# A third pair of token blocks in seven products, and the weights' conversion moved

## The chip, the cores and the metric

The kernel runs on one core of a Trainium2 chip. The metric is the device time of one execution in microseconds (us); lower is better. Five engines work side by side, each through its own instructions in order: TensorE (PE, matmuls), VectorE (DVE), ScalarE (ACT), GpSimd (POOL) and SyncE (SP, which here issues the DMAs).

## The reference

```python
# N = 6016 tokens, C = 256
qn = q / (norm(q, axis=tokens) + 1e-06);  kn = k / (norm(k, axis=tokens) + 1e-06)
s  = kn.T @ qn / tau                      # 256 x 256, over all tokens
a  = softmax(s);  x = v @ a               # 6016 x 256
h  = maximum(x @ w_in, 0);   x = (h * h) @ w_out              # first MLP, 256 -> 2048 -> 256
xn = x / sqrt(mean(x * x, -1) + 1e-06) * rms_g
g, val = xn @ w_gate, xn @ w_val                              # second MLP, 256 -> 1536
out = (g * sigmoid(g) * val) @ w_out2                         # 1536 -> 256
```

## The kernel before

Tokens are cut into 12 blocks (ten of 512, two of 448 columns), and blocks 2p and 2p+1 make pair p, p from 0 to 5. Features lie on the 128 partitions and tokens on the free axis. The scores come first, in a single pass over q and k; attention's matrix `a` is then multiplied into the first MLP's weights, so that the first MLP works on v directly with the operands `m_h`, `m_l`. Every float32 product is made of three matmuls of rounded parts, high by high, high by low, low by high (`mm3`, L109 to L112); what is "hi" below is a copy by ACT, what is "lo" the difference by DVE.

*First MLP.* A plain block runs 16 units, one for each 128 of the 2048 hidden features: a unit has 12 matmuls, six up and six down. A pair in the other form (`mlp1_pair`, L1310) runs 8 groups of two units for both its blocks. In place of eight 128-wide products (four combinations of feature half and input half, for two blocks) a group has seven products of sums and differences of the operands (`A11`, `S1`, ... `S4`), each of three matmuls, 21 for 24, followed by 24 down matmuls. `FIRST` is the first pair in this form: pairs 4 and 5 have it before. Its inputs are seven combinations of the pair's v, each as hi and lo. `v_steps` (L1198) forms them: load, transposes (L1219), differences (L1225, L1240), hi and lo. For the first such pair they stay on the chip (`first_place`), for the next they go through DRAM (`through_dram`) and come back by `fetch_v`. The weights' own sums and differences (`comb_steps`, 16 steps) are made beside the plain blocks, at the units that `COMB` names.

*Between the MLPs.* Each pair's output gets its norm (`pair_norm`, L976 to L1008: squares, a sum over 32 columns, a matmul with `mean_w`, the root, a reciprocal) and is formed into seven operands for the second MLP (`pair_steps`, stored to DRAM as `xd`). Both run as side steps (`side`, `aside`) of a later stage. A side step goes between two products of a group, so it stands in order on its engine among that group's own work.

*Second MLP.* Every pair runs 12 groups of seven products (L1458) and 12 down matmuls. After product 0, ACT copies its bank (L1511), and the next products accumulate onto that copy. The gate and value weights come as float64 halves, 256 columns of the 1536 in a chunk. A chunk takes a load (L134), a scaling on GpSimd and ACT (L142, L145), bit steps on DVE (L153, L157), for the value some sums on GpSimd, and a hi and lo of each piece; `gv_chunk(i)` is a chunk's tile of 1792 KB, and group f uses chunk f//2. Before, all six chunks are converted beside blocks 2 to 6: chunk 0 stays on the chip, and 1 to 5 go to DRAM and are loaded again (chunk 1 at L1766 after group 0 of the last MLP1 pair, 2 to 5 at L1828 after group 0 of the second MLP). The last rows of the second w_out (`late_calls`, tile `pu`) are loaded and converted beside MLP2's pair 0.

*Order.* The program order on each engine is written by hand. `CONV` says beside which blocks conversion steps run, `SKIP` which units take none. All DMAs that the change touches are issued by SP, in the order of the program; SP issues as soon as the waits of the DMA at its head are met.

Of the kernel before, what the change touches and what calls it, by code (L numbers as in the profile page):

```python
# [20 lines left out]
P = 128  # L21
# [7 lines left out]
def attn_moe_kernel(ctx: ExitStack, tc, q, k, v, tau, w_in, w_out, w_gate, w_val, w2, rms_g, out):  # L29
# [26 lines left out]
    FIRST = NP - 2  # L56
# [132 lines left out]
    EARLY = 3  # L189
    gv, gv_dram = {}, {}  # L190
# [11 lines left out]
    class Pieces(Call):  # L202


        def hi_of(self, j):
            src, x, k = self.pieces[j]
            if self.i < HELD:
                dst = gv_chunk(self.i)[:, :, x : x + k]
            else:
                dst = wp.tile([P, 2, 2, W2], F32R, tag="gp", name="gp", bufs=2)[:, :, :k]  # L210
            nc.scalar.copy(out=dst[:, 0], in_=src)
            self.made.append(dst)

        def lo_of(self, j):
# [3 lines left out]
            if self.i >= HELD:  # L218
# [8 lines left out]
        def h(self):  # L227
            self.made = []
            for j in range(self.np):
                self.hi_of(j)  # L230
                if self.i >= HELD:
                    self.lo_of(j)

        def l(self):
            if self.i < HELD:
# [162 lines left out]
    gv_calls = []  # L398
    for i in range(NGV):
        gate = Gate(cols(w_gate, i), i)  # L400
        gv_calls += [gate, Value(cols(w_val, i), i, gate)]
# [796 lines left out]
    def v_steps(p, into):  # L1198
# [11 lines left out]
        def tr(t, kk):  # L1210
            def f():
                if t == 0 and kk == 0:
                    x = vp.tile([P, KC, NB], F32, tag="vt", name="vt")[:, :, :n]
                    st["x"] = {0: x[:, 0], 4: x[:, 1], 5: x[:, 0]}
                if t == 1 and kk == 0:
# [72 lines left out]
    def fetch_v(p, i, ops):  # L1288
# [3 lines left out]
        if k < 6:  # L1292
# [10 lines left out]
    def mlp1_pair(p, ops, side, after_product, after_group):  # L1303
# [10 lines left out]
        def down(f, t, d, ph, pl, first, last):  # L1314
            def g():
# [115 lines left out]
    leftover, pw = [], []  # L1431

    def mlp2(p, ops, after_product, after_group, side):
# [17 lines left out]
        def group(f):  # L1451
            c = gv[f // 2]
# [235 lines left out]
    SKIP = {2: (), 3: (6, 9, 10), 4: (1, 5, 9, 13), 5: (3, 6, 8, 9), 6: (6, 9, 13, 15)}  # L1688
    COMB = {2: (4, 10, 14), 3: (12, 13, 14), 4: (8, 9, 11), 5: (0, 10, 12, 13, 14), 6: (11, 12)}
# [48 lines left out]

    ops0 = {}
# [4 lines left out]
    for p in range(FIRST, NP):  # L1744
        nxt = {}
        last = p == NP - 1
        if not last:
            tokens += v_steps(p + 1, through_dram(p + 1, first_stage))

        def after_product(g, i):  # L1750
            if g == NF1 // 2 - 1:
                if not last and i in ORDER[3:]:
                    fetch_v(p + 1, i, nxt)
                if last and i == 0:
                    fetch(0, 4, ops0)

        def after_group(g):
            if g == 0 and p > FIRST:
                side.extend(pair_norm(p - 1) + pair_steps(p - 1, staged("ys", "p0", "ys", "p1")))
# [4 lines left out]
            if last:  # L1764
                if g == 0:
                    nc.sync.dma_start(out=f32(gv_chunk(1)), in_=gv_dram[1])  # L1766
                if g == NF1 // 2 - 2:
                    assert not side, len(side)
# [122 lines left out]
```

## Time and profile before

| | |
|---|---|
| median of three runs | 1121.04 us (1120.5 to 1121.63) |
| the profiled execution | 1122.16 us |
| its span | 1120.5 us |
| PE busy | 1107.9 us, 99% |
| DVE, ACT busy | 779.8 and 789.6 us, 70% each |
| plain blocks 2 to 7, about | 188 to 437 us of the span |
| pairs 4 and 5 of the first MLP | 437 to 508, 508 to 577 |
| second MLP, pair 0 | 577 to 677; the later pairs about 90 us each |

The span is the time from the first to the last instruction of the profile; the execution's own time has 1.66 us more around it. A timeline row gives the start, the duration and the instruction; consecutive alike instructions are joined as "x6", and their duration then runs from the first start to the last end. An idle stretch ahead of a row stands in brackets with what ended it. Matmuls are pipelined: the next starts before the last has ended, so the pitch is the difference of two starts.

### The profile page before, as it was taken

What the parts mean: (1) busy time and instruction counts of PE and PEld (TensorE: products, weight loads), DVE (VectorE), ACT (ScalarE), POOL (GpSimd) and SP (SyncE); (2) the same over time, 40 slices, a digit from 0 to 9 for tenths busy, and PEclk for the clock granted to TensorE, in tenths of its full rate; (3) what the DMA queues carried; (4) which work ended last, traced back from release to release, by engine and by line L of the source; (5) the groups of instructions that cost most, each with busy time, mean ns of one, the idle gap of its engine ahead of it and who ended that gap; (6) DMA issues with size and microseconds to landing.
All of it is one profiled execution on the core that took longest, in us unless ns stands there. A gap on an engine that the chain in (4) does not pass through costs nothing.

```text
span 1120.5 us, 14578 instructions
## 1 busy us (share of the span) xinstructions
PE 1107.9 (99%) x5170; PEld 931.7 (83%) x5170; DVE 779.8 (70%) x1194; ACT 789.6 (70%) x1428; POOL 74.5 (7%) x106
## 2 busy tenths in 40 slices
PE   8999999999999999999999999999999999999997
PEld 7978888888888888888987888888888888888996
DVE  6998768887878787966857775555555655655655
ACT  7688778888888787777778666656566556556654
POOL 2521102202111000000000000000000000000000
PEclk9999999999999999999999999999999999999999
DMA  9633322362433331352276143102302302202001
GB/s 327 227 113 95 102 66 77 94 216 85 142 141 104 122 102 50 118 182 95 85 261 274 44 172 104 41 1 75 94 1 75 94 1 75 78 10 66 19 19 34
DMA packets 103305, 114.47 MB, mean 102 GB/s; under 512 B 50368, under 2 KB 71872, under 8 KB 102592
## 3 DMA queue, kind: packets, MB, share of 16 engines
q1 hardware_dynamic: 100960, 112.68, 29.8%
q10 hardware_dynamic: 2272, 0.85, 0.3%
q8 instruction: 41, 0.67, 0.2%
q14 instruction: 32, 0.26, 0.1%
HBM read 71.83 MB, written 41.68 MB: 101 GB/s over the span
## 4 chain that ended last, share of the span: by engine, by line
PE 90%; ACT 3%; DVE 2%; DMA 2%; POOL 1%; issue 1%; SPq 0%; DVEq 0%; ACTq 0%
PE mm L1458 29%; PE acc L110 13%; PE acc L112 13%; PE acc L111 13%; PE mm L1351 6%; PE mm L111 5%; PE mm L112 5%; PE mm L110 5%; POOL rows L569 1%; DMA qraw<-in_k_dram 1%; DMA rraw<-in_v_dram 1%; PE mm L761 1%; ACT ws L592 0%; ACT hl L609 0%; DVE dg L153 0%
## 5 line engine op out<-in xcount | busy, mean ns | idle before, releaser
L1458 PE MATMUL mm<-p,gv 128*128 128x512 f32 (+1 forms) x1188 | 302.6, 387 | 0.3 <-ACT mm L1511 0.3
L1458 PEld LDWEIGHTS mm<-p,gv 128*128 128x128 f32 x1188 | 221.6, 188 | 46.4 <-ACT mm L1511 1.4
L1561 DVE TENSOR_TENSOR sh<-hp,sh 128x512 fp32r<-128x512 f32 (+1 forms) x144 | 98.0, 681 | 139.6 <-ACT sh L1557 139.3
L1511 ACT COPY mm<-mm 128x512 f32<-128x512 f32 (+1 forms) x72 | 40.4, 561 | 171.0 <-PE mm L1458 161.9
L110 PE MATMUL acc<-sh,wo_h 128*128 128x512 f32 (+1 forms) x384 | 149.0, 388 | 0.0
L112 PE MATMUL acc<-sh,wo_l 128*128 128x512 f32 (+1 forms) x384 | 148.2, 386 | 0.2
L111 PE MATMUL acc<-sh,wo_h 128*128 128x512 f32 (+1 forms) x384 | 148.3, 386 | 0.0
L849 DVE TENSOR_TENSOR sh<-p,sh 128x512 fp32r<-128x512 f32 x128 | 92.8, 727 | 53.5 <-ACT sh L842 47.3
L110 PE MATMUL acc<-sh,w_h 128*128 128x512 f32 (+1 forms) x284 | 109.5, 386 | 0.0
L112 PE MATMUL acc<-sh,w_l 128*128 128x512 f32 (+1 forms) x284 | 109.5, 386 | 0.0
L111 PE MATMUL acc<-sh,w_h 128*128 128x512 f32 (+1 forms) x284 | 109.5, 385 | 0.0
L837 ACT ACTIVATE p<-mm 128x512 f32<-128x512 f32 x128 | 76.1, 594 | 27.6 <-PE mm L112 27.1
L1557 ACT CAST sh<-hp 128x512 fp32r<-128x512 f32 (+1 forms) x144 | 89.1, 619 | 3.2 <-DVE hp L1545 1.9
L112 PE MATMUL mm<-p,m_l 128*128 128x512 f32 x224 | 87.5, 391 | 0.3 <-DVE m_l L773 0.3
L110 PE MATMUL mm<-p,m_h 128*128 128x512 f32 x224 | 87.3, 390 | 0.0
L111 PE MATMUL mm<-p,m_h 128*128 128x512 f32 x224 | 87.2, 389 | 0.0
L112 PEld LDWEIGHTS acc<-sh,wo_l 128*128 128x128 f32 x384 | 72.1, 188 | 14.5 <-DVE wo_l L182 1.0
L111 PEld LDWEIGHTS acc<-sh,wo_h 128*128 128x128 f32 x384 | 72.1, 188 | 13.3 <-DVE sh L849 0.3
L110 PEld LDWEIGHTS acc<-sh,wo_h 128*128 128x128 f32 x384 | 72.1, 188 | 13.3 <-ACT wo_h L175 0.2
L1458 PE MATMUL mm<-xs,gv 128*128 128x512 f32 (+1 forms) x324 | 82.6, 381 | 0.0
L1545 DVE TENSOR_TENSOR hp<-mm,sg 128x512 f32<-128x512 f32 (+1 forms) x72 | 49.0, 680 | 43.3 <-PE mm L1458 42.9
L1536 DVE TENSOR_TENSOR hp<-mm,pu 128x512 f32<-128x512 f32 (+1 forms) x72 | 49.0, 681 | 30.2 <-ACT pu L1535 30.2
(249 smaller groups left out, 2078.8 us busy)
## 6 DMA issues: line engine op xcount, KB each, us to landing
p<-xd SPq DMA_DIRECT2D x58, 256.0 KB, 4.0
xd<-xp SPq DMA_DIRECT2D x40, 256.0 KB, 2.2
gv<-gvd SPq DMA_DIRECT2D x5, 1792.0 KB, 16.4
gvd<-gp SPq DMA_DIRECT2D x15, 512.0 KB, 3.3
xd<-p SPq DMA_DIRECT2D x30, 256.0 KB, 2.2
raw<-in_moe_w_out_dram SPq DMA_DIRECT2D x11, 512.0 KB, 3.6
out_dram<-ot SPq DMA_DIRECT2D x40, 128.0 KB, 2.3
qraw<-in_q_dram SPq DMA_DIRECT2D x13, 384.0 KB, 7.3
```

The costliest lines, as they stand in the source:

```text
L110: nc.tensor.matmul(o, wh, xh, start=start, stop=False)
L111: nc.tensor.matmul(o, wh, xl, start=False, stop=False)
L112: nc.tensor.matmul(o, wl, xh, start=False, stop=stop)
L837: nc.scalar.activation(out=r, in_=o, func=AF.Relu)
L849: nc.vector.tensor_tensor(out=sl, in0=s, in1=f32(sh), op=ALU.subtract)
L1351: nc.tensor.matmul(bank, m_part(a, w, g), x, start=start and j == 0, stop=j == 2, skip_group_check=not start)
L1458: nc.tensor.matmul(bank, c[:, hl, a, fs], x, start=start and j == 0, stop=j == 2, skip_group_check=not start)
L1511: cp(out=bu, in_=b0)
L1536: add(out=h22, in0=bh, in1=w, op=ALU.add)
L1545: dve(out=h21, in0=bv, in1=sg1, op=ALU.mult)
L1557: nc.scalar.copy(out=parts[t][0], in_=x)
L1561: dve(out=pl, in0=x, in1=f32(ph), op=ALU.subtract)
```

## The change

Pair 3 (blocks 6 and 7) takes the seven-product form too: `FIRST` goes from NP−2 to NP−3, and pairs 3, 4 and 5 have it. What goes with it:

- Conversion beside the plain blocks now ends with block 4, and only chunks 0 to 2 are converted there (`STREAMED = 3`); the 16 combination steps stand in blocks 2 to 4.
- Chunk 3 is converted beside the last MLP1 pair, in `vraw`, `dg`, `vt`, and staged through `p1` and `p6` to DRAM.
- Chunks 4 and 5 are converted beside pair 0 of the second MLP, straight into their tiles. Gate and value loads are new DMAs into tiles named `cr`.
- The operands of pair 5 take the tile `gv1` (as `vx`), so chunk 1's load moves from after group 0 of the last MLP1 pair to after product 1 of its last group.
- The last pair's MLP1 output is parked in DRAM (`yd`, four stores after group 1 of MLP2's pair 0), loaded back in pair 2 (`XLATE`), and its norm and operands are formed from group 3 of pair 2 on.
- `chunk_steps` is called with a list `early`. It is empty, so the loads are ordinary side steps, and `late_loads` is empty.

```diff
-    FIRST = NP - 2
+    FIRST = NP - 3
+    STREAMED = 3
@@ class Pieces
+        def direct(self):
+            return self.i < HELD or self.i > STREAMED
@@ def hi_of
-            if self.i < HELD:
-                dst = gv_chunk(self.i)[:, :, x : x + k]
-            else:
-                dst = wp.tile([P, 2, 2, W2], F32R, tag="gp", name="gp", bufs=2)[:, :, :k]
+            dst = gv_chunk(self.i)[:, :, x : x + k] if self.direct() else self.stage()[:, :, :k]
...
-    for i in range(NGV):
+    gv_calls = [c for i in range(STREAMED) for c in chunk_calls(i)]
@@ v_steps
+        wide = p > FIRST + 1
...
-                raw[t] = load_v(b + t)
+                raw[t] = load_v(b + t, place(0, F32) if wide else None)
...
+                if t == 0 and kk == 0 and wide:
+                    x = wp.tile([P, NC7, NB], F32, tag="gv1", name="vx")
@@ fetch_v
+        if k < 3 and p > FIRST + 1:
+            if k == 0:
+                ops["x"] = wp.tile([P, NC7, NB], F32R, tag="gv1", name="vx")
...
-    SKIP = {2: (), 3: (6, 9, 10), 4: (1, 5, 9, 13), 5: (3, 6, 8, 9), 6: (6, 9, 13, 15)}
-    COMB = {2: (4, 10, 14), 3: (12, 13, 14), 4: (8, 9, 11), 5: (0, 10, 12, 13, 14), 6: (11, 12)}
+    SKIP = {2: (4, 10, 14), 3: (4, 6, 9, 12, 13), 4: (1, 5, 9, 11, 13)}
+    COMB = {2: (2, 4, 6, 10, 14), 3: (0, 2, 12, 13, 14), 4: (2, 8, 9, 10, 11, 12)}
...
+    def chunk_steps(i, homes, early, stage=None):
+        calls2 = chunk_calls(i)
+        steps = []
...
+        gate, value = calls2
+        if early:
+            early.extend([gate.load, value.load])
+        else:
+            steps.append(gate.load)
+        for c in calls2:
+            after = [value.load] if c is gate and not early else []
+            steps += [only("act", c.a), only("dve", seq(c.b0, c.b1)), only("dve", seq(c.b2, *after))]
...
+            for j in range(c.np):
+                steps += [hi(j), only("dve", lambda c=c, j=j: c.lo_of(j))]
@@ the loop over the paired stages
-        if not last:
-            tokens += v_steps(p + 1, through_dram(p + 1, first_stage))
+        if last:
+            tokens += chunk_steps(
+                STREAMED, *shared_homes(), lambda t=cycle((1, 6)): place(next(t)).rearrange("p a (c w) -> p a c w", w=W2)
+            )
+        else:
+            tokens += v_steps(p + 1, through_dram(p + 1, stage if first else staged("p1", "ys")))
...
+                if last and i == 1:
+                    nc.sync.dma_start(out=f32(gv_chunk(1)), in_=gv_dram[1])
...
-                if g == 0:
-                    nc.sync.dma_start(out=f32(gv_chunk(1)), in_=gv_dram[1])
@@ beside the second MLP
-    x, y = rows_steps[1:], pair_side[6:]
-    side += pair_side[:5] + rows_steps[:1] + pair_side[5:6] + [f for i in range(max(len(x), len(y))) for f in x[i : i + 1] + y[i : i + 1]]
+    early, spare = [], {}
+    for i in range(STREAMED + 1, NGV):
+        chunk_side.append(chunk_steps(i, (gate_home, value_home), early))
+    late_loads = early[:2]
+    chunk_side[1][3:3] = [both(*early[2:])]
+    x, y = rows_steps, sum(chunk_side, [])
+    side += [f for i in range(max(len(x), len(y))) for f in x[i : i + 1] + y[2 * i : 2 * i + 2]]
...
-                    for i in (2, 3, 4, 5):
+                    for x in late_loads:
+                        x()
+                    for i in range(2, STREAMED + 1):
                         nc.sync.dma_start(out=f32(gv_chunk(i)), in_=gv_dram[i])
-            if f == 10 and p == 0:
+                if f == 1:
...
+                    for i in range(4):
+                        nc.sync.dma_start(out=y_dram[:, i, :nl], in_=x[:, 2 * i, :nl])
+            if p == XLATE:
...
+                if f == 3:
+                    side.extend(pair_side)
```

SP's queue at the start of the second MLP, before. `w_h` and `w_l` are rows of the second w_out, `gvd` the converted chunks in DRAM, `pu` the raw rows of the late w_out.

```order
L134 DMA pu<-in_moe_w_out_dram 128x2x512 [waits DMAHW0_49,PE_49]
L1808 DMA w_h<-w2d 128x1536 [waits DMAHW1_49,PE_49]
L1808 DMA w_l<-w2d 128x1536 [waits DMAHW2_49]
L1828 DMA gv<-gvd 128x3584 [waits DMAHW3_49]
L1828 DMA gv<-gvd 128x3584 [waits DMAHW4_49]
L1828 DMA gv<-gvd 128x3584 [waits DMAHW5_49,PE_49]
L1828 DMA gv<-gvd 128x3584 [waits DMAHW6_49,PE_49]
```

And the same place after the change:

```order
L134 DMA pu<-in_moe_w_out_dram 128x2x512 [waits DMAHW6_49,PE_49]
L1907 DMA w_h<-w2d 128x1536 [waits DMAHW7_49,PE_49]
L1907 DMA w_l<-w2d 128x1536 [waits DMAHW0_49]
L1933 DMA gv<-gvd 128x3584 [waits DMAHW1_49]
L1933 DMA gv<-gvd 128x3584 [waits DMAHW2_49]
L134 DMA cr<-in_moe_w_gate_dram 128x2x512 [waits DMAHW3_49,Pool_49]
L1938 DMA yd<-xst 128x448 [waits DMAHW4_49,Activation_49]
```

Two chunk loads of four remain, and the gate weights of chunk 4 stand behind them, ahead of the parked state's stores.

ACT's queue where group 1 of MLP2's pair 0 ends and group 2 begins, before:

```order
L1557 CAST sh<-hp 128x512 [waits DVE_49]
L1531 ACTIVATE sg<-mm 128x512 [waits PE_49]
L1535 COPY pu<-mm 128x512 [waits PE_49]
L976 ACTIVATE q<-xst 128x896 [waits DMAHW5_49,DMAHW4_49,Activation_49]
L145 ACTIVATE pu<-pu 128x512 [waits DMAHW0_49]
L1511 COPY mm<-mm 128x512 [waits DVE_49,PE_49]
```

After:

```order
L1578 CAST sh<-hp 128x512 [waits DVE_49]
L1552 ACTIVATE sg<-mm 128x512 [waits PE_49,Activation_49]
L1556 COPY pu<-mm 128x512 [waits PE_49]
L145 ACTIVATE cr<-cr 128x512 [waits DMAHW3_49]
L1532 COPY mm<-mm 128x512 [waits DVE_49,PE_49]
```

The norm's square has left this place; the conversion of the gate load stands where the conversion of the w_out rows was, which is now one group earlier.

DVE's queue in the only paired stage that has a norm beside it before, pair 5 (`p_4840` and `q` are the norm's; L1338 and L1341 the square and the low part of a group's activations; L1399 a sum of two banks):

```order
L981 TENSOR_TENSOR p_4840<-p_4840,q 128x1024
L984 STREAM_TRANSPOSE q<-p_4840 128x1024
L1338 TENSOR_TENSOR p_4015<-p_4014 128x448
L1341 TENSOR_TENSOR sh<-p_4015,sh 128x448
L987 TENSOR_REDUCE ns<-q 128x32
L1338 TENSOR_TENSOR p_4015<-p_4013 128x448
L1341 TENSOR_TENSOR sh<-p_4015,sh 128x448
L1399 ISA p_4013<-mm,sh 128x448
```

The same norm beside pair 4 after the change:

```order
L989 TENSOR_TENSOR p_4055<-p_4055,q 128x1024
L992 STREAM_TRANSPOSE q<-p_4055 128x1024
L1253 TENSOR_TENSOR xp<-vx,xp 128x448
L1357 TENSOR_TENSOR p_3219<-p_3218 128x512
L1360 TENSOR_TENSOR sh<-p_3219,sh 128x512
L995 TENSOR_REDUCE ns<-q 128x32
L1232 STREAM_TRANSPOSE vx<-p_4026 128x448
L1238 TENSOR_TENSOR vx<-vx 128x448
L1357 TENSOR_TENSOR p_3219<-p_3217 128x512
L1360 TENSOR_TENSOR sh<-p_3219,sh 128x512
L1418 ISA p_3217<-mm,sh 128x512
```

The group's own steps are the same, 512 columns wide; three steps of the next pair's preparation stand among them.

## Rows read from the trace of the kernel before

**Rows 1.** The page's first part: busy us, share of the span, instructions.

```profile
PE 1107.9 (99%) x5170; PEld 931.7 (83%) x5170; DVE 779.8 (70%) x1194; ACT 789.6 (70%) x1428; POOL 74.5 (7%) x106
```

**Rows 2.** The chain of waits: share of the span by engine.

```profile
PE 90%; ACT 3%; DVE 2%; DMA 2%; POOL 1%; issue 1%; SPq 0%; DVEq 0%; ACTq 0%
```

**Rows 3.** Windows: stretch, us, busy us of each engine, clock, DMA share, GB/s.

```profile
188.00:230.00 42.00, 42.00 (x188) 34.81 (x187) 38.12 (x54) 36.36 (x65) 12.47 (x13) 1.00 0.31 104
437.00:508.00 71.00, 71.00 (x317) 59.04 (x316) 55.20 (x90) 52.63 (x97) 0.00 (x0) 1.00 0.42 155
508.00:582.00 74.00, 73.96 (x359) 66.63 (x358) 54.02 (x88) 55.98 (x107) 0.15 (x1) 1.00 0.31 111
582.00:677.00 95.00, 94.70 (x414) 76.52 (x413) 67.79 (x109) 68.63 (x129) 1.97 (x3) 1.00 0.47 186
```

**Rows 4.** PE timeline in the second MLP's pair 1.

```profile
705.75 1.52 PE L1458 MATMUL mm<-p,gv 128*128 128x512 f32 x6
707.11 1.52 PE L1458 MATMUL mm<-xs,gv 128*128 128x512 f32 x6
708.47 0.39 PE L110 MATMUL acc<-sh,w_h 128*128 128x512 f32 x1
```

**Rows 5.** DVE timeline in pair 5 of the first MLP, with a norm.

```profile
521.91 1.22 DVE L981 TENSOR_TENSOR p<-p,q 128x1024 f32<-128x1024 f32 x1
523.16 1.25 DVE L984 STREAM_TRANSPOSE q<-p 128x1024 f32<-128x1024 f32 x1
...
530.89 0.63 DVE L1341 TENSOR_TENSOR sh<-p,sh 128x448 fp32r<-128x448 f32 x1 [2.06 <-ACT p L1336]
```

**Rows 6.** PE timeline in pair 5, matmuls of 448 columns.

```profile
531.48 0.36 PE L110 MATMUL acc<-sh,wo_h 128*128 128x448 f32 x1
531.68 0.37 PE L111 MATMUL acc<-sh,wo_h 128*128 128x448 f32 x1
531.89 0.37 PE L112 MATMUL acc<-sh,wo_l 128*128 128x448 f32 x1
```

**Rows 7.** DVE timeline in pair 4, a group without a norm.

```profile
450.84 0.63 DVE L1225 TENSOR_TENSOR p<-p,p 128x448 f32<-128x448 f32 x1
451.38 0.69 DVE L1341 TENSOR_TENSOR sh<-p,sh 128x512 fp32r<-128x512 f32 x1
```

**Rows 8.** PE timeline in pair 4, the matmul on that low part.

```profile
452.39 0.39 PE L111 MATMUL acc<-sh,wo_h 128*128 128x512 f32 x1
```

**Rows 9.** Issues at 579.5, 580.9, 585.0 us: KB each, us to landing.

```profile
pu<-in_moe_w_out_dram SPq DMA_DIRECT2D x1, 512.0 KB, 6.0
gv<-gvd SPq DMA_DIRECT2D x1, 1792.0 KB, 12.8
gv<-gvd SPq DMA_DIRECT2D x1, 1792.0 KB, 17.3
```

**Rows 10.** Windows at the end of pair 5, and after it.

```profile
573.00:580.00 7.00, 7.00 (x34) 5.98 (x33) 4.79 (x9) 5.97 (x11) 0.00 (x0) 1.00 0.55 181
580.00:602.00 22.00, 22.00 (x97) 17.35 (x96) 13.01 (x20) 17.35 (x30) 0.66 (x1) 1.00 1.01 411
```

**Rows 11.** ACT timeline around group 2 of the second MLP.

```profile
592.23 0.69 ACT L145 ACTIVATE pu<-pu 128x512 int32<-128x512 uint32 x1
594.17 0.57 ACT L1511 COPY mm<-mm 128x512 f32<-128x512 f32 x1 [1.25 <-DVE hp L1545]
```

**Rows 12.** PE timeline of the same stretch.

```profile
591.74 2.91 PE L1458 MATMUL mm<-p,gv 128*128 128x512 f32 x12
...
595.17 1.52 PE L1458 MATMUL mm<-p,gv 128*128 128x512 f32 x6
```

**Rows 13.** Windows after the last matmul.

```profile
1113.90:1117.70 3.80, 0.17 (x1) 0.00 (x0) 1.18 (x2) 0.00 (x0) 0.00 (x0) 1.00 0.79 190
1117.90:1120.50 2.60, 0.00 (x0) 0.00 (x0) 0.00 (x0) 0.00 (x0) 0.00 (x0) 0.50 0.26 57
```

**Rows 14.** PE timeline at the start of the span.

```profile
1.19 3.60 PE L584 MATMUL mm<-ws 128*128 128x512 bf16 x8 [1.19 <-DVE ws L580]
```

More of the change, by code (lines that the diff above doesn't have):

```diff
@@ L1211, in f @@
             def f():
-                if t == 0 and kk == 0:
+                if t == 0 and kk == 0 and wide:
+                    x = wp.tile([P, NC7, NB], F32, tag="gv1", name="vx")
+                    st["x"] = {i: x[:, i, :n] for i in range(NC7)}
+                elif t == 0 and kk == 0:
                     x = vp.tile([P, KC, NB], F32, tag="vt", name="vt")[:, :, :n]
                     st["x"] = {0: x[:, 0], 4: x[:, 1], 5: x[:, 0]}
-                if t == 1 and kk == 0:
+                elif t == 1 and kk == 0 and not wide:
                     a, c = (place(k, F32)[:, :, :n] for k in (0, 1))
@@ L1737, in attn_moe_kernel, with seq, g, hi @@
     assert not spill
+    formed = set()
+    def seq(*fs):
+        def g():
+            for f in fs:
+                f()
+        return g
+    def chunk_steps(i, homes, early, stage=None):
+        calls2 = chunk_calls(i)
+        steps = []
+        for c, home in zip(calls2, homes):
+            c.take = lambda c=c, home=home: c.__dict__.update(zip(("raw", "g"), home()))
+            if stage:
+                c.stage = stage
+        gate, value = calls2
[6 more added lines that the diff above has]
+            steps += [only("act", c.a), only("dve", seq(c.b0, c.b1)), only("dve", seq(c.b2, *after))]
+            def hi(j, c=c):
+                def f():
+                    if j == 0:
+                        c.made = []
+                    c.hi_of(j)
+                f = only("act", f)
+                f.staged = bool(stage)
+                return f
+            for j in range(c.np):
+                steps += [hi(j), only("dve", lambda c=c, j=j: c.lo_of(j))]
+        steps[-1] = only("dve", seq(steps[-1], lambda: formed.add(("gv", i))))
+        return steps
+    def flat_tile(pool, tag):
+        k = 2 if tag == "ys" else 1
+        return pool.tile([P, 2, NB], F32, tag=tag, name="cr", bufs=k)
+    def as_raw(t):
+        return t.rearrange("p a n -> p (a n)").bitcast(I32)
+    def shared_homes():
+        return (
+            lambda: (as_raw(flat_tile(vp, "vraw")), wp.tile([P, NB], F32, tag="dg", name="cg", bufs=3)),
+            lambda: (as_raw(flat_tile(vp, "vraw")), flat_tile(vp, "vt")[:, 0]),
+        ), []
     ops0 = {}
@@ L1746, in attn_moe_kernel @@
         last = p == NP - 1
-        if not last:
-            tokens += v_steps(p + 1, through_dram(p + 1, first_stage))
+        first = p == FIRST
+        stage = first_stage if first else staged("ys", "p0", "ys") if last else staged("ys", "p2")
+        if last:
+            tokens += chunk_steps(
+                STREAMED, *shared_homes(), lambda t=cycle((1, 6)): place(next(t)).rearrange("p a (c w) -> p a c w", w=W2)
+            )
+        else:
+            tokens += v_steps(p + 1, through_dram(p + 1, stage if first else staged("p1", "ys")))
         def after_product(g, i):
@@ L1764, in after_group @@
             if last:
[L1765 to L1766 removed]
                 if g == NF1 // 2 - 2:
[L1768 removed]
+                    assert not side and not tokens, (len(side), len(tokens))
                     for i in ORDER[:3]:
@@ L1810, in load_w2 @@
             )
+    XLATE = 2
+    nl = blocks[-1][1]
+    y_dram = dp.tile([P, 4, NB], F32, tag="yd", name="yd")
     ops, nxt, tails = ops0, {}, []
```

48 lines of the change are left out of this document (36 added, 12 removed).

## The prediction

> **What bounds the kernel now.** I read the busy line first: TensorE (PE) is busy 99% of the span, VectorE (DVE) and ScalarE (ACT) 70% each [rows 1]. The chain of waits says the same: 90% of the path that ended last is PE [rows 2]. The table by stage shows where that could change: PE has no gap worth naming in the plain blocks, the two paired stages and the first pair of the second MLP, and beside it DVE is at 78 to 91% in the first two and at 71 to 73% in the others, ACT at 72 to 87% [rows 3]. So a matmul that goes is worth its pitch, and what the other engines or a transfer do costs only where PE comes to wait for it. The pitch is the distance of starts, not the duration of one: twelve matmuls of 512 columns take from 705.75 to 708.47, 0.227 us each [rows 4].
>
> **The change, part by part.** The sum is made against the profiled execution: its own time is 1122.16 us, 1.12 above the median of 1121.04, and its span 1120.5. A sum of differences is added to the median.
>
> PE. Per pair, eight groups of 24 product matmuls in place of 2 × 8 × 12 up matmuls become eight of 21: 24 matmuls of 512 columns go. 24 × 0.227 = −5.45 us; with the small mean matmul of one norm −5.5. I see nothing that could take this back by itself.
>
> Blocks 2 to 4. Here DVE and ACT carry the same chunks' conversion and the combination steps squeezed from five blocks into three. A block is 16 × 12 × 0.227 = 43.6 us of PE. A block and its surroundings now show DVE 38.1 in 42.0 us [rows 3]; summed by the durations of their rows, the three blocks come to some 40, 41 and 38 us after. That still fits, so I take 0, with 1.0 as the upper end for one unit that bunches.
>
> Pair 4, now a middle pair. Its norm, 1024 wide, runs on DVE in front of the products' low parts, and now in the same stretch the next pair's preparation (L1232, L1238, L1253) stands between them. The only row where before does such a norm inside a paired stage is in the last pair: the two wide steps take 1.22 and 1.25 us, and the low part L1341 that follows the chain ends at 530.89 + 0.63 = 531.52 [rows 5], 0.16 us before the matmul that reads it, at 531.68 [rows 6]. Three added steps of 448 columns cost their spacing of 0.54 us each (450.84 to 451.38 [rows 7]), 1.6; the 512-wide forms of nine others some 0.06 each, 0.5. Against that a group of 45 matmuls is 45 × (0.227 − 0.205) = 1.0 longer than at 448 columns [rows 4, 6]. 1.6 + 0.5 − 1.0 − 0.16 = 0.9, say 1.0. The next group has the other half of the chain; a pair's group without a norm has 0.32 of slack (452.07 against 452.39 [rows 7, 8]), which one step more exceeds: 0.4. Together +1.4, from 0.3 (ACT, for which DVE idled 2.06 us in [rows 5], lets it catch up) to 3.0 (DVE's work of the two groups, 12.4 and 10.9 us by rows, against 10.2 us of PE each, all of it unhidden).
>
> Pair 5. The chunk's conversion puts one low part (some 0.6 us) into the same chain with its 0.16 of slack: +0.4, from 0 to 1.5.
>
> First pair of the second MLP, the large term. The new gate load of chunk 4 (512 KB) stands in SP's order behind w2_l and two chunk loads, and ACT's conversion of it (L145) stands directly ahead of group 2's first copy (L1532 now, L1511 before). ACT works in order, so that copy waits for the transfer, and PE's next products accumulate onto what the copy frees. When does it land? Before, the w_out load issued at 579.5 landed 6.0 later, at 585.5; the first chunk load, issued at 580.96, 12.8 later, at 593.8; the third, issued at 585.05, 17.3 later, at 602.3 [rows 9]. That is 4.27 us for each 1792 KB, with the 16 DMA engines full from 580 to 602 (share 1.01 at 411 GB/s [rows 10]). All of these land in the order of issue. Two chunk loads stand before the gate: 593.8 + 4.27 = 598.1. The load of chunk 1, moved from the start of pair 5 to right ahead of this burst, adds 4.27 of transfer; 0.45 × 7.0 = 3.2 us of free share lie in 573 to 580 [rows 10], so it pushes the burst by some 1.1. The gate's own 512 KB take 4.27 × 512/1792 = 1.2. It lands at 598.1 + 1.1 + 1.2 = 600.4, on before's clock.
>
> What needs it: before, L145 there ran at 592.23 for 0.69 us, on a load that had long landed, and the copy at 594.17 for 0.57 [rows 11]; the products followed at 595.17 [rows 12]. Now L145 ends at 601.1 and the copy at 601.6: PE resumes some 6.4 us late. Lower end 5.0 (the moved chunk hides wholly, and PE has 1.3 us more queued work than I count); upper end 8.5 (chunk 1's transfer is hidden by nothing). VectorE waits for the same transfer through GpSimd's scaled half, but its shift is behind the same products, 0.
>
> The Trainium skill speaks against this term ("DMA: Bandwidth & Descriptors", section "Queues, rings and completion order"): descriptors of one queue start in order but are pipelined over 16 engines, and nothing orders DMAs across these. By it the small gate load could end ahead of the chunks. The trace agrees only with order of issue in this burst, so I keep it as a rival.
>
> The w_out load and its L145, now ahead of group 1, landed at 585.5 where PE wanted the copy's input at about 587: 0, up to 1.0 with the push. The value load and chunk 5's loads are issued groups ahead of their use: 0. Parking and reloading pair 5's state are eight transfers of 224 KB with groups between: 0. The norm and its table loads move to MLP2 pair 2 at the same price: 0.
>
> The clock. After the last matmul the granted clock was still 1.00 in 1113.9 to 1117.7 and 0.50 in 1117.9 to 1120.5, with no matmul [rows 13]. It fell some 4 us after PE's last matmul, whose end the first of these stretches holds, and a stall of 6.4 us is longer. What a low clock costs is seen at the start: eight matmuls of 512 columns, the first work after idling, take 3.60 us to the end of the last [rows 14], about 0.427 each with the level at 1.2 GHz, where 2.4 GHz gives 0.227. If it recovers as there, after some 3.9 us, 3.9 × (1 − 0.227/0.427) = +1.8 us; from 0 (the gate doesn't fall) to 3.4 (it stays low twice as long).
>
> The Trainium skill says that the slow level is the default and that activity releases the fast one ("TensorE: Matmul & The Clock Gate", Part 1); by it a stall costs more than its length, as the tail's rows agree. Without it the sum is the same.
>
> Sum: −5.5 + 0 + 1.4 + 0.4 + 6.4 + 1.8 = **+4.5**, so 1121.0 + 4.5 = **1125.5 us**.
>
> **Rivals.** *The gate load lands in time.* If the load's packets pass the chunks', or ACT's L145 is not what the products wait for, the large term and the clock's go and −5.5 + 1.8 = −3.7 remains: 1117.3, faster. It decides when the load has landed by 593.9 (595.17 less 0.69 and 0.57), 6.5 us ahead of what the order of issue gives. For it: PE's slack behind group 1's twelve matmuls [rows 12]; against it: four landings in order at a full share [rows 9, 10]. 12%.
>
> *A short stall.* The load lands late, but the stall stays near 5.0, the clock holds, and the pairs lose little: −5.5 + 5.0 + 0 + 1.0 = +0.5 to +2.0, 1121.5 to 1123.0: no change. For it: the clock outlasts four idle us in the tail. 21%.
>
> *VectorE overloaded in the pairs.* The low parts fall behind in groups 1 to 3 of pair 4 and again in pair 5, at their upper ends 3.0 + 1.5 in place of 1.8: 1125.5 + 2.7 = 1128.2, slower. For it: DVE's 0.16 us of slack [rows 5, 6]; against it: its idle 2.06 us just ahead. It decides once the wide chain has no idle gap to shrink. 12%.
>
> *The saving doesn't come*: the seven products need as many copies and low parts as PE waits for. Against it: pair 4 before has them at PE 71.00 of 71.00 us [rows 3]. 2%, at 1131.
>
> **How the numbers follow.** Forecast 53% (own range 1123.3 to 1127.5), rivals 12, 21, 12 and 2. Differences within 0.2% (1118.8 to 1123.3) can't be told from no change. Faster: the first rival and a little of the second, 13%; same: the second, 21%; slower: the forecast, the third and the fourth, 66%. For 8 in 10 the range leaves out the deeper half of the faster case and the last case: 1118.5 to 1128.5.
>
> **What would show it.** An idle stretch of PE of 5 to 8 us at MLP2's group 2, ended by ACT's first copy after L145 on a tile filled from the gate weights; that DMA landing 13 to 20 us after its issue, behind both chunk loads; the granted clock at 0.5 or between in the us after it. In pair 4, waits of L111 for the low part L1360, of 0.3 to 3 us in all; blocks 2 to 4 without any. If PE runs through group 2, the large term is wrong; if pairs 4 and 5 lose over 3 us, the third rival holds; if PE runs at full pitch right after the stall, the clock's term is wrong.

## The result, and the profile after

The changed kernel takes 1136.97 us (median of 4 runs, 1134.68 to 1138.47), the kernel before 1121.34 beside it: ratio 1.0135, 95% interval 1.0113 to 1.0157. It is slower, as forecast, but by 15.6 us and not by 4.5, and outside the range. The profiled execution took 1136.62 us, its span 1134.8, 14.3 more than before.

TensorE (PE) is as busy as before [rows 1], with 26 matmuls fewer; the page's first part:

```profile
PE 1109.5 (98%) x5144; PEld 928.0 (82%) x5144; DVE 797.9 (70%) x1224; ACT 789.5 (70%) x1431; POOL 71.3 (6%) x104
```

Most of what came on top is waiting: PE stands idle for 25.3 us of the span, 12.6 before. Its busy time grew by 1.6 us where fewer matmuls should have cut it by 5.5: the matmuls beside a wait start further apart, some ran at the low clock, and the last pair at a slower pitch (told at the end). The table takes each stage from the start of its first product to the start of the next stage's first, in both traces; the last column is the prediction's term. Of the −5.82, 0.42 stood already at 184 us, ahead of all that was changed.

| stage | before | after | difference | predicted |
|---|---|---|---|---|
| up to pair 4 | 420.56 | 414.74 | −5.82 | −5.5 |
| pair 4 | 81.93 | 84.41 | +2.48 | +1.4 |
| pair 5 | 75.46 | 79.56 | +4.10 | +0.4 |
| MLP2 pair 0 | 91.47 | 103.63 | +12.16 | +8.2 |
| MLP2 pairs 1 to 4 | 359.56 | 359.92 | +0.36 | 0 |
| MLP2 pair 5, to the last matmul's end | 85.09 | 86.41 | +1.32 | 0 |
| sum | 1114.07 | 1128.66 | +14.6 | +4.5 |

(One correction: pair 4's first product starts at 420.6 before and pair 5's at 502.5, not at 437 and 508 as the first part has it; its second window in [rows 3] ends inside pair 5.) The same stages in the windows of after, where a row's first busy time is PE's and the clock stands behind the engines:

```profile
414.70:499.10 84.40, 83.41 (x363) 67.12 (x363) 66.95 (x104) 63.73 (x114) 0.00 (x0) 1.00 0.36 125
499.10:578.70 79.60, 76.03 (x365) 67.59 (x365) 61.82 (x100) 59.10 (x114) 5.41 (x6) 1.00 0.38 136
578.70:682.30 103.60, 93.37 (x397) 74.56 (x396) 65.96 (x106) 63.15 (x121) 12.10 (x16) 0.97 0.39 154
602.20:609.00 6.80, 3.52 (x8) 2.81 (x9) 3.13 (x6) 4.07 (x8) 1.44 (x2) 0.50 0.60 230
```

Before, PE was idle there for 0.3 us in all [rows 3]; now 1.0, 3.6 and 10.2 us are idle in the first three, and the granted clock is 0.50 in the fourth, from late in the longest gap on. What PE waited for (total us, times, longest):

```profile
PE mm L1479 <- ACT mm L1532: 6.5, 2, 6.1
PE mm L1479 <- DMA p<-xd: 2.4, 1, 2.4
PE acc L111 <- DVE sh L1360: 2.2, 3, 1.0
...
PE mm L999 <- DVE ns L995: 1.5, 2, 1.2
PE mm L1479 <- ACT pu L1556: 1.3, 2, 0.9
...
PE acc L110 <- ACT sh L1351: 0.7, 1, 0.7
```

The longest is the one that was forecast. PE at the start of the second MLP, where [rows 12] ran on:

```profile
586.52 1.02 PE L1479 MATMUL mm<-p,gv 128*128 128x512 f32 x3 [2.42 <-DMA p<-xd]
...
591.98 2.58 PE L1479 MATMUL mm<-p,gv 128*128 128x512 f32 x9 [0.45 <-ACT mm L1532]
...
605.48 2.93 PE L1479 MATMUL mm<-p,gv 128*128 128x512 f32 x6 [6.10 <-ACT mm L1532]
608.21 0.63 PE L110 MATMUL acc<-sh,w_h 128*128 128x512 f32 x1
```

And ACT beside it, against [rows 11]:

```profile
604.28 0.67 ACT L145 ACTIVATE cr<-cr 128x512 int32<-128x512 uint32 x1 [8.72 <-DMA cr<-in_moe_w_gate_dram]
604.85 0.58 ACT L1532 COPY mm<-mm 128x512 f32<-128x512 f32 x1
```

L145 stands 8.7 us on its transfer, the copy follows, PE resumes. Six matmuls then take 2.93 us where [rows 4] show 1.52. Four of the issues in this burst, at 575.6, 579.6, 580.3 and 588.3 us (KB, us to landing; the first is chunk 1, the last the gate weights):

```profile
gv<-gvd SPq DMA_DIRECT2D x1, 1792.0 KB, 10.3
p<-xd SPq DMA_DIRECT2D x1, 256.0 KB, 9.9
pu<-in_moe_w_out_dram SPq DMA_DIRECT2D x1, 512.0 KB, 10.5
cr<-in_moe_w_gate_dram SPq DMA_DIRECT2D x1, 512.0 KB, 15.9
```

SP's queue shows why the gate load was issued so late:

```profile
580.29 0.38 SPq L134 DMA_DIRECT2D pu<-in_moe_w_out_dram  x1
585.96 0.32 SPq L1907 DMA_DIRECT2D w_h<-w2d  x1
586.40 0.36 SPq L1907 DMA_DIRECT2D w_l<-w2d  x1
```

The w2 rows stood 5.7 us at the head of the queue, until chunk 1's load had landed (575.6 + 10.3 = 585.9), and six operand loads and the w_out rows lay behind that load. The prediction saw the load's bytes, but only in front of the gate; they cost an operand first: the six operand loads behind chunk 1 landed after 9.5 to 10.0 us.

The operand loads were late for a second reason. Ahead of the first eight, SP stood at the last store of chunk 3's conversion, which waits for that chunk's last low part. Before, and after:

```profile
566.80 12.63 SPq L1124 DMA_DIRECT2D p<-xd  x14
```

```profile
570.69 0.53 SPq L225 DMA_DIRECT2D gvd<-p  x1
571.32 4.18 SPq L1132 DMA_DIRECT2D p<-xd  x8
```

So they went out 7.4 us ahead of the second MLP's first product (578.70), and before 11.2 us ahead of it (577.95). The DMA engines have no room left in 573 to 580 us, where [rows 10] show a share of 0.55:

```profile
573.00:580.00 7.00, 7.00 (x34) 6.08 (x34) 4.73 (x8) 5.85 (x11) 0.00 (x0) 1.00 1.05 360
```

In pair 5, the low part L221 of chunk 3 stands between the norm's transpose and its reduction (L995), and PE waits for the reduction:

```profile
523.50 0.65 DVE L221 TENSOR_TENSOR p<-cg,p 128x512 fp32r<-128x512 f32 x1
...
525.34 1.21 DVE L995 TENSOR_REDUCE ns<-q 128x32 f32<-128x1024 f32 x1
```

```profile
526.69 0.38 PE L999 MATMUL mm<-ns,mean_w 128*128 128x32 f32 x2 [1.18 <-DVE ns L995]
```

### The profile page after: what moved, and what is told of

The parts are those of the page before. It is cut to its first block, busy times and chain, and to the rows that moved or that the text cites. A ratio compares the mean times of both kernels' runs of the same rounds, so it can differ in the third digit from the quotient of the medians.

```text
span 1134.8 us, 14551 instructions
## 1 busy us (share of the span) xinstructions
PE 1109.5 (98%) x5144; PEld 928.0 (82%) x5144; DVE 797.9 (70%) x1224; ACT 789.5 (70%) x1431; POOL 71.3 (6%) x104
## 5 line engine op out<-in xcount | busy, mean ns | idle before, releaser
L1479 PE MATMUL mm<-p,gv 128*128 128x512 f32 (+1 forms) x1188 | 304.9, 389 | 10.2 <-ACT mm L1532 6.5
L857 DVE TENSOR_TENSOR sh<-p,sh 128x512 fp32r<-128x512 f32 x96 | 68.7, 715 | 37.2 <-ACT sh L850 33.2
L112 PEld LDWEIGHTS acc<-sh,wo_l 128*128 128x128 f32 x384 | 72.1, 188 | 14.3 <-DVE wo_l L182 1.0
L1479 PE MATMUL mm<-xs,gv 128*128 128x512 f32 (+1 forms) x324 | 82.9, 382 | 0.0
L1360 DVE TENSOR_TENSOR sh<-p,sh 128x512 fp32r<-128x512 f32 (+1 forms) x95 | 64.4, 678 | 21.9 <-ACT p L1355 11.3
L845 ACT ACTIVATE p<-mm 128x512 f32<-128x512 f32 x96 | 57.1, 595 | 20.7 <-PE mm L112 20.2
L1479 PEld LDWEIGHTS mm<-xs,gv 128*128 128x128 f32 x324 | 60.8, 188 | 10.6
L1351 ACT ACTIVATE sh<-p 128x512 fp32r<-128x512 f32 (+1 forms) x95 | 58.3, 614 | 13.6 <-DVE p L1418 12.0
```

The costliest lines, as they stand in the source:

```text
L112: nc.tensor.matmul(o, wl, xh, start=False, stop=stop)
L845: nc.scalar.activation(out=r, in_=o, func=AF.Relu)
L857: nc.vector.tensor_tensor(out=sl, in0=s, in1=f32(sh), op=ALU.subtract)
L1351: nc.scalar.activation(out=st["h"], in_=r, func=AF.Square)
L1360: nc.vector.tensor_tensor(out=st["l"], in0=q, in1=f32(st["h"]), op=ALU.subtract)
L1479: nc.tensor.matmul(bank, c[:, hl, a, fs], x, start=start and j == 0, stop=j == 2, skip_group_check=not start)
```

## The experiments

Each ratio is to the kernel before on the same chip; the changed kernel stands at 1.0135 (1.0113 to 1.0157). "After" means the changed kernel's trace. Diffs show the main lines of an edit; "..." marks what is cut.

**gate_first: the gate load ahead of the chunks.**

```diff
-            steps.append(gate.load)
+            hoist = i == STREAMED + 1
+            steps.append((lambda: None) if hoist else gate.load)
+            if hoist:
+                hoisted.append(gate.load)
...
-    late_loads = early[:2]
+    late_loads = hoisted
```

> The changed kernel (1137.0 us) with one DMA moved: the gate load of chunk 4 is issued ahead of the two chunk loads, its place among the side steps is left empty. Theory A (transfers land in order of issue, and this load lies behind 3.6 MB): it lands at about 595.5 in place of 604.25, the idle 6.1 us of TensorE at group 2 and the 1.75 us of low clock behind it go: -7.8, 1129.2 us. Rival B (the path through ScalarE's L145 is late for another reason, or the load of chunk 1 and the w_out rows end later still): the stall stays over 3 us and the time over 1132.

Measured 1.0066 (1.0053 to 1.0079). The load now lands after 10.1 us, at 597.8, and group 2 has no wait. At group 3 the next load in the queue, the value of chunk 4, is late (issued at 596.5, 13.3 to landing):

```profile
cr<-in_moe_w_gate_dram SPq DMA_DIRECT2D x1, 512.0 KB, 10.1
...
611.06 1.22 PE L1479 MATMUL mm<-p,gv 128*128 128x512 f32 x2 [2.30 <-ACT mm L1532]
```

Theory A holds for this load, but not for the gain: pair 0 takes 99.4 us for 103.6, since 0.9 us came on w_l and 2.3, with a fall of the clock, at group 3. So 4.2 us of the 7.8 came. That the ratio is near the expected one all the same is owed to 1.3 us in the last pair, told at the end, and for the rest to chance, as far as the traces show.

**gv1_after_fetch: chunk 1 behind the operands.**

```diff
-                if last and i == 1:
-                    nc.sync.dma_start(out=f32(gv_chunk(1)), in_=gv_dram[1])
...
                     for i in (2, 5, 6):
                         fetch(0, i, ops0)
+                    nc.sync.dma_start(out=f32(gv_chunk(1)), in_=gv_dram[1])
```

> The changed kernel (1137.0 us) with the load of chunk 1 issued after the second MLP's last operand loads in place of ahead of six of them. Theory A (one backlog: the queue is never empty from 575 to 604, so the bytes in front of the gate load stay the same): the 2.4 us wait for an operand at the start of the second MLP goes, but the gate load still lands near 604 and the stall at group 2 grows by as much: 0 to -0.5, 1136.5 us. Rival B (each wait has its own price): -2.4 to -3.0, 1134 us.

Measured 1.0123 (1.0107 to 1.0138), no difference that the interval shows. The gate load was issued 3.5 us earlier, at 584.8, and landed 0.7 us later, at 604.9 (604.25 in after):

```profile
cr<-in_moe_w_gate_dram SPq DMA_DIRECT2D x1, 512.0 KB, 20.1
```

and PE's waits in that stretch are

```profile
592.50 2.58 PE L1479 MATMUL mm<-p,gv 128*128 128x512 f32 x9 [2.91 <-ACT mm L1532]
...
606.14 1.22 PE L1479 MATMUL mm<-p,gv 128*128 128x512 f32 x2 [6.24 <-ACT mm L1532]
```

The operand's 2.4 us went and 2.9 came at group 1, behind the w_out rows. Theory A had the place of the return wrong (group 2) and the sum right: the queue is never empty, so a byte taken from before one load stands before another. The gate load landed no earlier for being issued earlier.

**edf: the loads by due time.** Operands, w_out rows, w2 rows, gate of chunk 4, chunk 1, value of chunk 4, chunks 2 and 3:

```diff
...
+                    for x in late_loads[:1]:
+                        x()
+                    nc.sync.dma_start(out=f32(gv_chunk(1)), in_=gv_dram[1])
+                    for x in late_loads[1:]:
+                        x()
...
```

> The changed kernel (ratio 1.0135 to the kernel before) with four loads put in the order of their due times at the start of the second MLP: last operands, w_out rows, w2 rows, gate of chunk 4, chunk 1, value of chunk 4, chunks 2 and 3. The shorter run gate_first left waits of 0.8 us on an operand, 0.9 on w_l, 0.5 behind the w_out rows and 2.3 at group 3, behind the value load. Theory A (one queue served in order, each load late by the bytes ahead of it): all four go, the clock stays up, pair 0 of the second MLP takes 91.5 plus some 1.5 us for VectorE's waits in place of 103.6: -10.5, ratio 1.0040. Rival B (the transfers of this stretch together are more than its time, so a wait stays wherever they are put): pair 0 still takes over 96 us, ratio over 1.007.

Measured 1.0042 (1.0029 to 1.0056), expected 1.0040 (1.3 us of the gain is the last pair's pitch). MLP2's pair 0 takes 95.9 us for 103.6 (theory A: 93, rival B: over 96). One transfer is still late, chunk 1's, and the clock falls once behind it:

```profile
596.29 2.93 PE L1479 MATMUL mm<-p,gv 128*128 128x512 f32 x6 [2.05 <-DMA gv<-gvd]
```

So theory A stands with a remainder of B: 2.05 us that this order leaves. All four waits that theory A names are gone.

**chunk3_load: chunk 3's gate load 8 us earlier.**

```diff
...
+                if p == NP - 2 and i == 1:
+                    hoisted.pop(0)()
...
```

> The changed kernel (1137.0 us) with one DMA moved: chunk 3's gate load is issued in the last group of pair 4, ahead of the next pair's operands, its place among the side steps is left empty. Theory A (ScalarE's L145 waited 2.0 us for this load at 509 and held the group's squares behind it): TensorE's two waits at 510 and 511, 1.8 us with the pitch, go, and nothing else in pair 5: -1.8, 1135.2 us. Rival B (VectorE and ScalarE have too much work in that group whatever the load does): the waits stay within 0.5, 1137 us.

In after, ACT's L145 waits here for a load of 5.5 us, and PE behind it twice:

```profile
509.15 0.68 ACT L145 ACTIVATE cr<-cr 128x512 int32<-128x512 uint32 x1 [2.01 <-DMA cr<-in_moe_w_gate_dram]
```

```profile
510.33 0.47 PE L110 MATMUL acc<-sh,wo_h 128*128 128x448 f32 x1 [0.73 <-ACT sh L1351]
511.46 0.47 PE L111 MATMUL acc<-sh,wo_h 128*128 128x448 f32 x1 [0.66 <-DVE sh L1360]
```

Measured 1.0109 (1.0095 to 1.0122), by the time alone not to be told from 1.0135. Both waits are gone from the trace, so theory A has their cause; the gain is smaller, since 0.5 us (0.9 with the pitch) came on pair 5's operands, now behind the moved load. Pair 5 takes 79.1 us for 79.6, in this run at the slower of the two pitches told at the end, which hides some 0.7 us of the gain.

**no_sums: without GpSimd's sums for chunks 3 to 5.**

```diff
             add = nc.gpsimd.tensor_tensor
-            add(out=s[:, 0], in0=a2[:, 0], in1=a2[:, 1], op=ALU.add)
+            if self.i < STREAMED:
+                add(out=s[:, 0], in0=a2[:, 0], in1=a2[:, 1], op=ALU.add)
...
```

> The changed kernel (1137.0 us) without GpSimd's four sums of the value weights for chunks 3 to 5 (the combinations of those weights are left out, the raw halves stand in their place; all other instructions stay). Theory A (while GpSimd sums, VectorE's instructions take about twice as long: 1.16 for 0.62 us at 537): VectorE keeps 0.6 us, TensorE's waits at 538 (1.15) and 626 (1.05) go and that at 642 stays: -2.2, 1134.8 us. Rival B (VectorE is behind there because of the number of its instructions): the waits stay, 1137 us.

Measured 1.0091 (1.0077 to 1.0105). In after, DVE beside the sums, and the sums:

```profile
535.17 0.97 DVE L1360 TENSOR_TENSOR sh<-p,sh 128x448 fp32r<-128x448 f32 x1
536.06 1.23 DVE L1021 SCALAR_TENSOR_TENSOR xst<-xst,few,p 128x512 f32<-128x512 f32 x1
537.21 1.16 DVE L1357 TENSOR_TENSOR p<-p 128x448 f32<-128x448 f32 x1
```

```profile
535.62 1.12 POOL L302 TENSOR_TENSOR cr<-cg,cr 128x256 f32<-128x256 f32 x1
536.70 1.18 POOL L303 TENSOR_TENSOR cr<-cr,cg 128x256 f32<-128x256 f32 x1
```

The same three on DVE without them:

```profile
535.49 0.63 DVE L1361 TENSOR_TENSOR sh<-p,sh 128x448 fp32r<-128x448 f32 x1
536.03 0.75 DVE L1022 SCALAR_TENSOR_TENSOR xst<-xst,few,p 128x512 f32<-128x512 f32 x1
536.69 0.62 DVE L1358 TENSOR_TENSOR p<-p 128x448 f32<-128x448 f32 x1
```

0.34 to 0.54 us each is what the sums take from DVE, and PE's waits at 538 and 626 are gone with them: theory A. Pair 5 and MLP2's pair 0 fell by 1.1 us each (to 78.5 and 102.6), the 2.2 that were expected; in pair 0 other waits changed too, about as much up as down. Of the rest of the span's 3.8, 1.3 is the last pair's pitch, told below. The Trainium skill has this rule ("SBUF — State Buffer", section "SBUF: two separate sides"): a VectorE instruction with two SBUF inputs and a GpSimd instruction that reads SBUF exclude each other. The trace agrees: DVE's instructions take up to twice as long, and the sums L302 and L303, which take 0.73 and 0.92 us at 658 us of the same trace, take 1.12 and 1.18 here.

**chunk3_in_blocks: chunk 3's conversion back beside blocks 2 to 4.**

```diff
-    STREAMED = 3
+    STREAMED = 4
-    SKIP = {2: (4, 10, 14), 3: (4, 6, 9, 12, 13), 4: (1, 5, 9, 11, 13)}
+    SKIP = {2: (14,), 3: (13,), 4: (9,)}
...
```

> The changed kernel with the conversion of chunk 3 taken from pair 5 back to the plain blocks 2 to 4, where 45 of 48 units now have a conversion step (35 before). Theory A (pair 5 lost its 4.1 us to this chunk's steps; the blocks have room, 40, 41 and 38 us of VectorE in 43.6): pair 5 takes 75.5 us, the blocks lose under 1 us, -3.5, ratio 1.0104. Rival B (the blocks are full: the ten more steps put VectorE behind): pair 3 starts 3 us or more later and the time doesn't change.

Measured 1.0113 (1.0099 to 1.0126). Pair 5 takes 74.8 us for 79.6, below the kernel before's 75.5: chunk 3 was all that it lost. But pair 3 starts at 339.5 for 332.6:

```profile
248.70 0.80 PE L110 MATMUL mm<-p,m_h 128*128 128x512 f32 x1 [2.56 <-ACT p L106]
...
258.18 0.50 PE L111 MATMUL acc<-sh,wo_h 128*128 128x512 f32 x1 [1.09 <-DVE sh L857]
```

Both theories in part: A for pair 5, where PE has no gap left, B for the blocks, where the ten steps cost some 6 us (2.6 and 1.1 of waits, and a clock of 0.5 for 3.4 us). MLP2's pair 0 gained 2.2 us (101.5), which neither theory had: chunk 3's store is gone from SP's queue, the first operand loads go out 10.9 us ahead of MLP2 (580.91), and PE no longer waits for an operand, though chunk 1's load still stands ahead of six of them.

```profile
570.02 3.72 SPq L1132 DMA_DIRECT2D p<-xd  x8
```

That the ratio lies near theory A's 1.0104 is chance: the profiled execution is made of −4.8, −2.2 and −1.3 (the last pair's pitch) against +6.9.

**hold: group 2 of pairs 4 and 5 left to the norm.**

```diff
-                for q in [side] * k + [tokens]:
+                for q in [side] * k + [tokens] * (1 if p == FIRST or g < 2 else 0 if g == 2 else 2):
```

> The changed kernel with the preparation steps of pair 4 and the conversion steps of pair 5 left out of group 2, where the norm's sum and mean matmul stand, and made up from group 3 on, two at a time. Theory A (TensorE waits there because these steps stand in VectorE's order ahead of the norm's reduction and of the low parts): the waits for the reduction (0.4 and 1.2 us) and the one at 447 (0.55) go, -2.5 with their pitch, pairs 4 and 5 take 83 and 78 us. Rival B (the later groups have no room either): the same waits come back from group 3 on, 0 to +1.

Measured 1.0157 (1.0143 to 1.0171); pair 4 took 85.2, pair 5 86.4 us. In pair 4 the wait of 0.55 went and one of 0.73 came at 457: rival B, and more than it said. The waits for the reduction stayed at 0.36 and 1.17 us, but on them the run decides nothing: the step that stands ahead of the reduction runs at the end of group 1, which the edit doesn't touch, and it is still there (L992, the transpose, ends at 528.08; L995 starts at 529.83):

```profile
528.00 0.65 DVE L221 TENSOR_TENSOR p<-cg,p 128x512 fp32r<-128x512 f32 x1
```

The doubled steps put ACT behind DVE (L215 on a tile that L221 releases), and PE behind both:

```profile
553.71 1.02 PE L1370 MATMUL mm<-vr,c 128*128 128x448 f32 x2 [2.40 <-ACT mm L1406]
```

**no_diffs: pair 5's preparation without its four differences.**

```diff
+                if not wide:
+                    nc.vector.tensor_tensor(out=st["x"][o], in0=st["x"][x], in1=st["x"][y], op=ALU.subtract)
...
-                nc.scalar.copy(out=st[i][0], in_=st["x"][i])
+                nc.scalar.copy(out=st[i][0], in_=st["x"][from_(i)])
```

> The changed kernel (ratio 1.0135) without the four differences of VectorE in the preparation of pair 5's v beside pair 4 (the seven operands are made from the four transposed parts alone). Theory A (pair 4's 2.4 us are VectorE's lateness under norm and preparation together): 2.2 us of its work less, so pair 4 takes 83 us in place of 84.4, ratio 1.0122. Rival B (it is the chain of the norm, ScalarE to VectorE to TensorE, that is late by itself): pair 4 stays at 84.4.

Measured 1.0106 (1.0092 to 1.012). Pair 4 takes 82.9 us for 84.4, and the 0.55 us on the low part (in after, below) is gone; the 0.36 on the reduction stays. Theory A for 1.5 of 2.5 us.

```profile
441.80 0.38 PE L999 MATMUL mm<-ns,mean_w 128*128 128x32 f32 x2 [0.36 <-DVE ns L995]
...
448.04 0.50 PE L111 MATMUL acc<-sh,wo_h 128*128 128x512 f32 x1 [0.55 <-DVE sh L1360]
```

**combined: the edits of edf, chunk3_in_blocks and hold.**

> All three together: loads in order of due times, chunk 3 in the blocks, group 2 of pairs 4 and 5 left to the norm. If each works as its theory A says, the changed kernel's +14.6 us become about -2 to +0.5: 14.6 - 10.5 - 3.5 - 1.5 = -0.9, ratio 0.999. If the losses only move (the rivals), the ratio stays over 1.005.

Measured 1.0104 (1.0091 to 1.0118). MLP2's pair 0 took 94.1 us, but `hold` delayed pair 5's operands (PE waits 2.26 us for them at its start, and the clock falls), and the blocks lost as before: the rivals' case.

**edf_load3 and edf_load3_spread: the edits of edf and chunk3_load together, and GpSimd's sums one per side step.**

```diff
...
+            sums.pop(0)()
+            if self.i < STREAMED:
+                for f in sums:
+                    f()
+            else:
+                self.sums = sums
...
+                    if c is not gate and c.sums:
+                        c.sums.pop(0)()
...
```

> The loads in the order of due times as in edf (ratio 1.0042), and chunk 3's gate load in the last group of pair 4 as in chunk3_load. Theory A (the late load's 1.8 us in pair 5 and the loads' waits at the second MLP are separate): -1.8 from edf, ratio 1.0026. Rival B (pair 5 is short of VectorE and the wait moves to its next group): ratio 1.004.

Measured 1.0038 (1.0025 to 1.0051). The times don't separate it from edf. In the traces pair 5 takes 79.2 us for edf's 79.9, but that is no gain of the edit: edf ran it at the slower pitch, and of the waits 0.37 and 0.65 us went while 1.07 came on pair 5's operands, behind the moved load. Pair 0 takes 1.7 us less: chunk 1 is late by 1.64, and the clock doesn't fall behind that gap. Theory A is not borne out; the wait moved, though not to the place that rival B names.

> As edf_load3, and GpSimd's four sums of chunks 3 to 5 one at a time, each beside another side step, in place of four in a row. Theory A (four in a row slow some six instructions of VectorE to about double, which outruns the slack of one group; one at a time fits it): the waits of 1.15 us in pair 5 and 1.05 and 0.5 in the second MLP go, -2.4 from edf_load3, ratio 1.0005. Rival B (the slowed instructions cost the same wherever they stand): no change from edf_load3.

Measured 1.0032 (1.002 to 1.0044). The waits stayed (1.02 and 0.89 us), because the sums still ran in a row:

```profile
534.83 1.00 POOL L303 TENSOR_TENSOR cr<-cr,cg 128x256 f32<-128x256 f32 x1
535.79 1.18 POOL L304 TENSOR_TENSOR cr<-cg,cr 128x256 f32<-128x256 f32 x1
...
```

GpSimd has nothing else to do there and their inputs are ready, so a later place in the program held nothing back. The run doesn't decide between its theories.

**direct3_spread: chunk 3 too beside MLP2's pair 0.**

```diff
-            tokens += chunk_steps(
-                STREAMED, *shared_homes(), lambda t=cycle((1, 6)): place(next(t)).rearrange("p a (c w) -> p a c w", w=W2)
-            )
+            pass
...
-    for i in range(STREAMED + 1, NGV):
+    for i in range(STREAMED, NGV):
         chunk_side.append(chunk_steps(i, (gate_home, value_home), early))
...
+                    for x in loads_of[STREAMED]:
+                        x()
...
```

> Chunk 3 isn't converted beside pair 5 but, as 4 and 5, beside the second MLP's pair 0, straight into its tile; its raw halves are loaded at the end of pair 5, each later chunk's loads follow the bit steps of the one before, chunk 1 is loaded behind the w2 rows, the sums stand one at a time, and pair 0 takes one more side step per group. Theory A (pair 5 loses only by chunk 3's steps, 4.1 us, and the second MLP's pair 0 has room on VectorE, 71% busy): pair 5 takes 75 us, pair 0 under 94, ratio 0.999 to 1.001. Rival B (pair 0 has no room for another 6 us of VectorE and 5 of ScalarE work): pair 0 over 97 us, ratio over 1.003.

Measured 1.0067 (1.0054 to 1.0079): pair 5 takes 74.6 us, pair 0 102.8. Rival B; ACT's casts wait for DVE's bit steps and hold the copies behind them, at five groups, as in

```profile
622.30 2.19 PE L1488 MATMUL mm<-p,gv 128*128 128x512 f32 x6 [2.18 <-ACT mm L1541]
```

No version that was run beats the kernel before.

## Why the prediction was wrong

*The saving* was right: −5.82 (−5.4 without the 0.42 from the start) for −5.5, with blocks 2 to 4 at no cost. The last rival is out.

*The gate load* was right in mechanism: 6.1 us idle for 6.4, ended by the copy behind L145 on that tile. That the size fits is partly luck. The landing came 3.9 us later than worked out (604.25 for 600.4), and PE arrived 4.1 us later too (599.23 for 595.17): 0.8 of either is that the second MLP began later, the rest is the same full queue, which held PE twice before it came to group 2. The load never passed another one: in this burst all land in the order of issue, also when a load is moved in it, so the faster rival and the Trainium skill's warning ("DMA: Bandwidth & Descriptors", section "Queues, rings and completion order") that order isn't given did not come into play here.

*The clock* was right in size: 0.50 from 602.2 to 609.0, and the eight matmuls that started in it took 1.7 us more than at 0.227 each, for 1.8. Its reason was not: it fell 2.8 us after PE's last matmul and not some 4, and other runs show falls behind shorter gaps (last section), so the tail's 4 us were no bound, and the second rival could not lean on them.

*Step that failed, first: "Pair 5 ... the chunk's conversion puts one low part (some 0.6 us) into the same chain ... +0.4, from 0 to 1.5".* It cost 4.1 us. I counted one of the chunk's 15 steps. That one is there: L221 stands ahead of the norm's reduction, for which PE waits 1.18 us; this wait goes with the chunk in chunk3_in_blocks, but what part of it is L221's and what a bit step's ahead of it was not isolated. Two mechanisms were left out, and the runs show both: ACT's L145 on a load issued one step before (0.73 and 0.66 us, gone in chunk3_load), and GpSimd's sums beside DVE (0.99, gone in no_sums). That the first of them is the mechanism I priced at 6.4 us in the second MLP, one stage later, is the plainer half of the miss.

*Second: the push of 1.1 us by chunk 1's load, and where it was applied.* It counted on 3.2 us of free share in 573 to 580; that stretch was full. And it was priced only for the gate and the w_out load (0.45 us at group 1, inside its 1.0). Six operand loads of 256 KB were issued behind chunk 1, landed after 9.5 to 10.0 us in place of 4, and PE waited 2.4 us for one; no term stood for that. The wait hangs on the moved load and on chunk 3's store ahead of the operand loads: it was gone when either was taken away (gv1_after_fetch; chunk3_in_blocks, where the chunk's other steps went too). In four runs that leave this order (gate_first, chunk3_load, no_sums, no_diffs) it was 0.85 to 1.54 us. edf, which puts all by due time, takes 7.7 us off pair 0; chunk 1's wait (2.05) with its low clock, one wait beside the sums (0.89) and one of 0.25 are what is left.

*Third, a size: pair 4*, +2.5 for +1.4, inside its bounds of 0.3 to 3.0. no_diffs shows 1.5 of it to be the preparation's load on DVE. The rival that had VectorE overloaded in both pairs holds by the sign that the prediction gave it (over 3 us; 6.6 were lost), and the steps ahead of the norm's reduction are its mechanism; but in pair 5 three of the four waits hang on a load and on GpSimd's sums, which it did not have.

*Not a step at all*: MLP2's pair 5, +1.3 us, and 0.6 for the norm now beside its pair 2, which was set at the price that it had before.

## What to carry to other kernels

Price a moved load by everything that is issued behind it, and price every step of a moved piece, not the one that stands in the chain you look at, its last store in the DMA queue too: here the first conversion step stood on its own load twice, and only one was counted. When one queue was full from end to end, taking one load forward only named another as the late one (gate_first, gv1_after_fetch); what helped was order by due time. Fewer bytes were not tried.

## What the runs showed of the hardware

- The granted clock fell to 0.50 around gaps of PE of 2.05, 2.26, 2.30 and 2.40 us as well (edf, combined, gate_first, hold) and stayed there for 3.4 us, but not around gaps of 2.42 us (after, at 586) and 2.91 us (gv1_after_fetch, at 592). Beyond the gap itself the low level cost 1.6 to 1.7 us in after, edf and gate_first, and 2.6 in gv1_after_fetch behind its gap of 6.24. By the Trainium skill ("TensorE: Matmul & The Clock Gate", Part 1) the slow level is the default and activity releases the fast one. The runs agree so far that a gap can cost more than its length; which gap does could not be told from its length.
- Matmuls of 448 columns ran a whole stage at one of two pitches, about 0.203 or 0.207 us, at a granted clock of 1.00. Before, pair 5 of the first MLP had the slower and MLP2's pair 5 the faster; after, it was the other way round. Of the other runs edf, gate_first and chunk3_load had the slower in pair 5, gv1_after_fetch and chunk3_load in MLP2's pair 5. That is the +1.3 us there. It also hides 0.7 to 0.9 us of pair 5's loss: with no gap and at the faster pitch pair 5 took 74.8 and 74.6 us (chunk3_in_blocks, direct3_spread), so the loss is nearer 5 us at like pitch. Its cause was not tried.

```profile
1029.00:1103.00 74.00, 74.00 (x364) 67.89 (x363) 42.67 (x71) 44.42 (x92) 0.00 (x0) 1.00 0.10 29
```

```profile
1042.30:1117.60 75.30, 75.30 (x364) 67.95 (x363) 42.89 (x71) 44.73 (x92) 0.00 (x0) 1.00 0.10 29
```

The rows show 74.0 us for 364 matmuls of that stage before, and 75.3 us for 364 after, both with no gap.
